# Summing kv in fewer runs, a second place for the last projections, and a new instruction order, in a linear-attention + SoLU feed-forward kernel

## The chip, the cores and the metric

The kernel runs on one core of one Trainium2 chip. The metric is device microseconds (us) of one execution; a run before the change took 510.22 us (median of 3 runs, 509.39 to 512.36). TensorE is called PE, VectorE DVE, ScalarE ACT, GpSimd POOL and SyncE SP, as in the profile. All transfers are issued from SP.

## The reference

Two stages, all in float32 at the interface. Batch 8, 8 heads, sequence 576, head size 64; the hidden width is 1024.

```python
def _attn_ref(q, k, v):
    q_s = softmax(q over the head dimension)        # exp(q - max) / (sum + 1e-9)
    k_s = softmax(k over the sequence)              # the same over 576 positions
    kv = np.einsum('bhsd,bhse->bhde', k_s, v)       # 64 x 64 for each head
    return np.einsum('bhsd,bhde->bhse', q_s, kv)

def _moe_ref(x, w_in, w_out, g_ln):                 # x: 4608 rows of 512
    h = x @ w_in                                    # 4608 x 1024
    e = np.exp(h - max(h)); sm = e / (sum(e) + 1e-9)
    solu = h * sm
    ln = (solu - mean) / np.sqrt(var + 1e-6) * g_ln
    return ln @ w_out                               # 4608 x 512
```

## The kernel before, in words

The sequence of each batch is cut into four full tiles of 128 rows (`C = 4`) and a rest of 64 rows; the rests of two neighbouring batches share one row tile, so there are 36 row tiles for 8 batches. The work is a set of Python generators, each of which issues a few instructions and yields:

- `K0` to `K7` (`keys(b)`): column maxima of k, subtraction, exponential, then the sum kv into one PSUM tile. Its matmuls are `km` by `vm` (128 rows contracted, line 375) and, for the 64 rest rows, `kr` by `vr` (line 377). For each of the four pairs of heads the eight full-tile matmuls are followed at once by the two rest matmuls, and then the generator yields. `largest` transposes a maximum (line 154) and two steps write kv into the block-diagonal weights `bd` (lines 395 and 397). These operands have four bytes per element, and the trace records each such matmul twice.
- `V..` loads v and casts it to `vm`; `Q..a`, `Q..b`, `Q..c` and `R..` make the softmax of q (lines 414 to 432) and transpose it by DMA.
- `w..`, `W` and `y..`, `Z` turn the weights, which arrive as 8-byte numbers, into pairs of float16 (lines 238 to 312).
- `x<t>` (`attend`) multiplies q by `bd`; `h<t>` (`hidden`) is the first feed-forward matmul, 24 matmuls of 128x512 into `h`, of which PSUM holds two, and the row-wise work on it: maximum (DVE line 529), exponential (ACT), small scalars `am`, `pi`, `p`, `ph` (mostly POOL, lines 539 to 548), product (DVE line 551), two halves of `u` (ACT line 556, DVE line 558), its transposition by DMA to `uT`, and the sum of squares (ACT line 565), after which `h` is free.
- `o<t>` (`project`) is the second feed-forward matmul, 24 matmuls of 128x512 into `o`; then DVE or ACT scales it into `os` (lines 601 and 603) and SP stores it. The pool tag `o` has one buffer. The tag `att` has three, used by `x`, `kv` and the transposed maxima. The last row tile is projected in two halves of 256 columns.

The string `ORDER` lists the steps one by one: `h3` runs generator `h3` to its next yield, `K0*2` does that twice, and the ending `.v` gives to DVE the operation that is otherwise POOL's or ACT's (`on(...)`). Each engine and SP work through their instructions in the order in which the list issues them, so an instruction that waits holds up all behind it on its engine. `P` is a step of idle matmuls at the start.

Of the kernel before, what the change touches and what calls it, by code (L numbers as in the profile page):

```python
# [8 lines left out]
F32 = mybir.dt.float32  # L9
# [8 lines left out]
P = 128  # L18
# [66 lines left out]
)  # L85


@with_exitstack
def linear_attention_solu_ffn(ctx: ExitStack, tc: tile.TileContext, q, k, v, w_in, w_out, g_ln, out):

# [6 lines left out]
    nc = tc.nc  # L97
    B, H, S, D = q.shape
# [4 lines left out]
    C = 4  # L103
# [10 lines left out]
    ps = ctx.enter_context(tc.tile_pool(name="ps", bufs=1, space=bass.MemoryType.PSUM))  # L114
# [10 lines left out]
    vm = cst.tile([P, H, C, D + 1], F32, name="vm")  # L125
# [210 lines left out]
    def keys(b):  # L336
# [3 lines left out]
        km = raw["km"]  # L340
# [372 lines left out]
```

## Time and profile before

| | |
|---|---|
| runs shown | 510.22 us median, 509.39 to 512.36 |
| profiled execution, its own time | 510.97 us |
| its span, first to last instruction | 509.2 us |
| PE busy | 463.3 us, 91% of the span |
| DVE busy | 374.5 us, 74% |
| ACT, POOL busy | 279.7 us, 197.5 us |
| DMA | 74.98 MB, 147 GB/s over the span |

Busy time says how long an engine was executing, not whether it set the time. A row of the window view gives, for a stretch of the span, the busy microseconds of each engine and the granted TensorE clock; a row of the timeline view gives start, length, engine, line and operation, with the idle time before it and what ended that in square brackets. Consecutive equal instructions are merged (x16), and the lengths of matmuls overlap, so that the pace of PE is read from starts.

### The profile page before, as it was taken

To read this page: it belongs to the slowest core of one execution; us is meant where nothing else is said; L and a number is where in the kernel's file an instruction comes from. 1 tells how busy PE (TensorE), PEld (TensorE's weight loads), DVE (VectorE), ACT (ScalarE), POOL (GpSimd) and SP (SyncE) were. 2 spreads that over 40 slices of the span, in tenths; PEclk is the share of its full clock that TensorE was granted. 3 is DMA by queue.
4 is the path that set the end of the run, shared out by engine and by line. 5 is a ranking of instruction groups with operands and counts; after the bars stand their busy time and mean duration, and the time that the engine had idled before them with its cause. 6 is when DMAs were issued, how large, how long until landed. Compare 5 with 4: busy or idle time off the path is not lost.

```text
span 509.2 us, 7977 instructions
## 1 busy us (share of the span) xinstructions
PE 463.3 (91%) x2990; PEld 235.3 (46%) x2990; DVE 374.5 (74%) x618; ACT 279.7 (55%) x457; POOL 197.5 (39%) x293
## 2 busy tenths in 40 slices
PE   7357875999999999899999999999999999999986
PEld 2223442445555545454455455545554544444434
DVE  3999999999898989778867777788765464342521
ACT  2657387848557476845547557546656444333400
POOL 3312278457353264753164536326415122020110
PEclk9567997999999999999999999999999999999999
DMA  8896777439996949668729757793626333422251
GB/s 271 246 228 219 220 193 185 103 41 211 213 203 175 217 87 219 139 118 229 161 52 222 205 124 167 149 224 84 132 65 131 74 90 59 103 43 62 60 128 41
DMA packets 159239, 74.98 MB, mean 147 GB/s; under 512 B 127840, under 2 KB 152672, under 8 KB 159200
## 3 DMA queue, kind: packets, MB, share of 16 engines
q1 hardware_dynamic: 159200, 74.47, 62.1%
q8 instruction: 23, 0.38, 0.3%
q14 instruction: 16, 0.13, 0.1%
HBM read 36.70 MB, written 9.44 MB: 91 GB/s over the span
## 4 chain that ended last, share of the span: by engine, by line
PE 59%; DVE 25%; issue 6%; ACT 4%; DMA 3%; POOL 1%; SPq 0%; DVEq 0%; POOLq 0%; ACTq 0%
PE o L593 29%; PE h L522 23%; DVE u L558 3%; PE kv L375 2%; DVE bd L397 2%; DMA w_out<-in_moe_w_out_dram 2%; DVE top L529 1%; DVE qsum L421 1%; DVE qnmx L414 1%; ACT u L556 1%; DMA kr<-in_k_dram 1%; DVE khalf L347 1%; DVE wo L312 1%; DVE iw L242 1%; PE kv L377 1%
## 5 line engine op out<-in xcount | busy, mean ns | idle before, releaser
L522 PE MATMUL h<-wi,xT 128*128 128x512 f16 x864 | 204.9, 384 | 9.5 <-ACT e L565 8.5
L593 PE MATMUL o<-wo,uT 128*128 128x512 f16 (+1 forms) x888 | 200.2, 373 | 4.3 <-DVE os L601 4.1
L522 PEld LDWEIGHTS <-xT 128*128 128x128 f16 x864 | 84.1, 99 | 108.3 <-issue 14.9
L593 PEld LDWEIGHTS <-uT 128*128 128x128 f16 x888 | 85.7, 98 | 99.7 <-issue 5.9
L529 DVE TENSOR_REDUCE top<-h 128x1 f32<-128x1024 f32 x36 | 43.8, 1216 | 33.8 <-PE h L522 33.8
L558 DVE SCALAR_TENSOR_TENSOR u<-h,nmu,u 128x1024 f16<-128x1024 f32 x36 | 46.1, 1280 | 18.3 <-ACT u L556 18.2
L551 DVE SCALAR_TENSOR_TENSOR h<-h,ph,e 128x1024 f32<-128x1024 f32 x36 | 46.3, 1287 | 12.8 <-POOL ph L548 10.7
L539 POOL TENSOR_SCALAR am<-nm 128x1 f32<-128x1 f32 x25 | 9.2, 367 | 111.5 <-ACT nm L531 111.4
L565 ACT ACTIVATE e<-h,nmu 128x1024 f32<-128x1024 f32 x36 | 40.0, 1112 | 19.0 <-DVE u L558 18.9
L556 ACT ACTIVATE u<-h,nmu 128x1024 f16<-128x1024 f32 x36 | 40.0, 1111 | 0.9
L531 ACT ACTIVATE nm<-top,hs 128x1 f32<-128x1 f32 x32 | 9.4, 294 | 55.6 <-DVE top L529 55.4
L535 ACT ACTIVATE e<-h,nm,hs 128x1024 f32<-128x1024 f32 x32 | 38.5, 1203 | 0.8
L432 POOL TENSOR_TENSOR qhl<-qm,qhl 128x1024 f16<-128x1024 f32 (+1 forms) x13 | 28.2, 2169 | 22.2 <-ACT qhl L148 19.4
L553 ACT ACTIVATE nmu<-s 128x1 f32<-128x1 f32 x36 | 7.3, 202 | 52.7 <-DVE h L551 52.6
L578 POOL TENSOR_TENSOR r<-var,mhalf 128x1 f32<-128x1 f32 x36 | 23.2, 649 | 27.4 <-DVE var L575 26.6
L545 POOL TENSOR_TENSOR p<-pi,mone 128x1 f32<-128x1 f32 x36 | 21.7, 602 | 26.1 <-DVE pi L542 24.4
L601 DVE TENSOR_SCALAR os<-o,rr 128x512 f32<-128x512 f32 (+1 forms) x16 | 11.4, 715 | 27.1 <-PE o L593 27.1
L427 POOL TENSOR_TENSOR qm<-qm,qrec 128x1024 f32<-128x1024 f32 x11 | 21.7, 1975 | 20.7 <-DVE qrec L425 14.3
L375 PE MATMUL kv<-vm,km 128*64 128x65 f32 x512 | 23.7, 238 | 5.0 <-ACT vm L148 2.6
L473 PE MATMUL x<-qT,bd 128*128 128x128 f16 x128 | 24.1, 225 | 4.2 <-DVE bd L397 4.2
L375 PEld LDWEIGHTS kv<-vm,km 128*64 128x64 f32 x512 | 19.0, 147 | 14.0 <-issue 4.6
L507 DVE SCALAR_TENSOR_TENSOR xT<-x,xT 128x512 f16<-128x512 f32 x36 | 24.6, 682 | 1.2 <-ACT xT L505 1.2
(137 smaller groups left out, 663.4 us busy)
## 6 DMA issues: line engine op xcount, KB each, us to landing
v<-in_v_dram SPq DMA_DIRECT2D x32, 256.0 KB, 3.6
out_dram<-os SPq DMA_DIRECT2D x31, 256.0 KB, 3.2
km<-in_k_dram SPq DMA_DIRECT2D x7, 1024.0 KB, 6.2
qm<-in_q_dram SPq DMA_DIRECT2D x7, 1024.0 KB, 6.3
w_in<-in_moe_w_in_dram SPq DMA_DIRECT2D x8, 512.0 KB, 6.5
w_out<-in_moe_w_out_dram SPq DMA_DIRECT2D x8, 512.0 KB, 5.7
out_dram<-os SPq DMA_DIRECT2D x10, 128.0 KB, 2.4
km<-in_k_dram SPq DMA_DIRECT2D x2, 512.0 KB, 4.4
```

The costliest lines, as they stand in the source:

```text
L375: nc.tensor.matmul(o, km[:, h + i, c], vm[:, h + i, c], start=(c == 0), stop=False)
L432: on(nc.gpsimd).tensor_tensor(lo, x, hi, op=ALU.subtract)
L473: nc.tensor.matmul(acc, al, bh, start=False, stop=True)
L507: nc.vector.scalar_tensor_tensor(xT[:, 1], acc, 1.0 / QS, xT[:, 0], op0=ALU.mult, op1=ALU.subtract)
L522: nc.tensor.matmul(h[:, ns], xT[:, t, kc], wi[:, s, kc, ns], start=(i == 0), stop=(i == len(terms) - 1))
L529: nc.vector.tensor_reduce(top, h, axis=AX.X, op=ALU.max, negate=True)
L535: nc.scalar.activation(e, h, AF.Exp, bias=nm, scale=hs, accum_out=z)
L551: nc.vector.scalar_tensor_tensor(h, h, ph, e, op0=ALU.mult, op1=ALU.mult, accum_out=s1)
L556: nc.scalar.activation(u[:, 0], h, AF.Identity, bias=nmu)
L558: nc.vector.scalar_tensor_tensor(u[:, 1], h, nmu, u[:, 0], op0=ALU.add, op1=ALU.subtract)
L565: nc.scalar.activation(e, h, AF.Square, bias=nmu, accum_out=s2)
L593: nc.tensor.matmul(o, uT[:, j, f], wo[:, s, f, cols], start=(f == 0 and j == 0 and s == 0), stop=(f == NF - 1 and j == 1))
```

## The change

It does three things.

1. `keys`: the full-tile matmuls of four heads are issued together, then those of the other four, then the rest matmuls of all heads: three steps instead of four. The first matmul alone starts the sum.
2. `project`: of the last six row tiles, every other one (and the first half of the very last) takes its `o` from the three `att` buffers instead of the single `o` buffer.
3. `ORDER` is another list: 1721 steps instead of 1728, with 151 endings `.v` instead of 163. Of its table one row of before and one of after stand below. The order in which the weights are loaded, the order of the queries, the interleaving of all steps and the engine of several steps differ.

```diff
 ORDER = (
-    "LK0*3 w3 K0*2 w3 V00 LQ0 K0*3 P*4 K0*3 LQ0 w0*2 K0 w3 V00 K0.v LV0 w3 K0 w3 K0.v w3 K0*2 Q0a Q0b w0 "
...
+    "LK0*3 LQ0 K0*4 LQ0 K0 P*4 K0*2 w3 Q0c w3 K0*4 V00 w3 Q0a Q0a.v V03 V00 K0.v w0*2 Q0a Q0c V01 K0 Q0b "
...
 )
...
-        for h in range(0, H, 2):
-            for c in range(C + 1):
-                for i in range(2):
-                    o = acc[i * D : (i + 1) * D, h // 2]
-                    if c < C:
-                        nc.tensor.matmul(o, km[:, h + i, c], vm[:, h + i, c], start=(c == 0), stop=False)
-                    else:
-                        nc.tensor.matmul(o, kr[rows, h + i], vr[rows, h + i], start=False, stop=True)
-            yield
+        for hs in heads:
+            for h in range(hs.start, hs.stop, 2):
+                for c in range(C):
+                    for i in range(2):
+                        o = acc[i * D : (i + 1) * D, h // 2]
+                        nc.tensor.matmul(o, km[:, h + i, c], vm[:, h + i, c], start=(h == 0 and c == 0), stop=False)
+            yield
+        for h in range(0, H, 2):
+            for i in range(2):
+                o = acc[i * D : (i + 1) * D, h // 2]
+                nc.tensor.matmul(o, kr[rows, h + i], vr[rows, h + i], start=False, stop=(h == H - 2))
+        yield
...
+    LATE = B * S // P - 6
...
-            o = ps.tile([P, w], F32, name=f"o{name}{i}", tag="o", bufs=1)
+            o_tag = "att" if t >= LATE and (t + i) % 2 else "o"
+            o = ps.tile([P, w], F32, name=f"o{name}{i}", tag=o_tag, bufs=3 if o_tag == "att" else 1)
```

First place: PE, the kv sum of batch 1 (tile `kv1`), before. A row `x8` is eight matmuls in a row.

```order
L375 MATMUL kv1_635<-vm_76,km1_299 64x65 x8
L377 MATMUL kv1_635<-vr_77,kr0_100 64x65 x2
L375 MATMUL kv1_635<-vm_76,km1_299 64x65 x8
L377 MATMUL kv1_635<-vr_77,kr0_100 64x65 x2
L375 MATMUL kv1_635<-vm_76,km1_299 64x65 x8
L377 MATMUL kv1_635<-vr_77,kr0_100 64x65 x2
L375 MATMUL kv1_635<-vm_76,km1_299 64x65 x8
L377 MATMUL kv1_635<-vr_77,kr0_100 64x65 x2
```

The same place on PE now, with the row before it and the two behind it.

```order
L526 MATMUL h0_2_571<-wi_67,xT0_2_533 128x512
L376 MATMUL kv1_626<-vm_76,km1_317 64x65 x32
L381 MATMUL kv1_626<-vr_77,kr0_100 64x65 x8
L153 MATMUL kv1_626<-ident_86,mx1_700 128x128
L526 LDWEIGHTS xT0_3_619
```

Eight runs of one kind have become two. In batches 2 to 7 the steps are spread between other matmuls; there the 48 runs have become 15: two runs of full tiles and one of rests in batches 2, 4 and 6, one of each in batches 3, 5 and 7.

Second place: PE where the projection of row tile (7, 0) ends and the next begins, before.

```order
L593 LDWEIGHTS uT7_0_4881
L593 MATMUL o7_00_5155<-wo_68,uT7_0_4881 128x512
L593 LDWEIGHTS uT7_1_4985
L593 MATMUL o7_10_5199<-wo_68,uT7_1_4985 128x512
L593 LDWEIGHTS uT7_1_4985
```

The same engine now, where the projection of row tile (7, 1) in the `o` buffer ends; `o7_20` lies in an `att` buffer and `o7_40` in the `o` buffer.

```order
L600 MATMUL o7_10_5232<-wo_68,uT7_1_4949 128x512
L600 LDWEIGHTS uT7_2_5092
L600 MATMUL o7_20_5214<-wo_68,uT7_2_5092 128x512
L600 LDWEIGHTS uT7_2_5092
L600 MATMUL o7_20_5214<-wo_68,uT7_2_5092 128x512
```

Between two users of the `o` buffer there are now matmuls of a tile in another buffer: six of `o7_20` here, then `o7_40` begins.

Third place: POOL, its first operations on whole tiles, before (`km`: k; `qm`: q; `qhl`: the float16 halves of q).

```order
L358 TENSOR_TENSOR km0_97<-km0_97,kb0_152 128x1024
L416 TENSOR_TENSOR qm0_111<-qm0_111,qnmx0_1_168 128x8x64
L432 TENSOR_TENSOR qhl0_0_229<-qm0_111,qhl0_0_229 128x512
L480 TENSOR_TENSOR hs0_439<-inv_kv0_338,isc_75 128x1
L432 TENSOR_TENSOR qhl0_2_365<-qm0_111,qhl0_2_365 128x8x2x64
L542 TENSOR_SCALAR pi0_0_491<-am0_0_487 128x1
```

And POOL now, from the same start.

```order
L357 TENSOR_TENSOR km0_97<-km0_97,kb0_149 128x1024
L420 TENSOR_TENSOR qm0_102<-qm0_102,qnmx0_2_141 128x8x128
L420 TENSOR_TENSOR qm0_102<-qm0_102,qnmx0_1_172 128x8x64
L431 TENSOR_TENSOR qm0_102<-qm0_102,qrec0_0_184 128x8x64
L431 TENSOR_TENSOR qm0_102<-qm0_102,qrec0_1_240 128x8x64
L436 TENSOR_TENSOR qhl0_0_232<-qm0_102,qhl0_0_232 128x512 x2
L431 TENSOR_TENSOR qm0_102<-qm0_102,qrec0_2_273 128x8x128
L484 TENSOR_TENSOR hs0_421<-inv_kv0_306,isc_75 128x1
L543 TENSOR_SCALAR am0_0_487<-nm0_0_462 128x1
```

Four more operations on whole tiles of the first batch have gone from DVE to POOL; over the program POOL has 62 of them instead of 53.

123 rows, old and new, of the table ORDER are left out of this document.

## Prediction

> **What bounds the kernel now.** I read the page first, then the windows of 20 us, then the waits of PE, then the timeline of PE where the change acts. The windows give, in order, PE, PEld, DVE, ACT and POOL busy, the granted TensorE clock, the DMA share and GB/s.
>
> ```profile
> PE 463.3 (91%) x2990; PEld 235.3 (46%) x2990; DVE 374.5 (74%) x618; ACT 279.7 (55%) x457; POOL 197.5 (39%) x293
> ...
> 20.00:40.00 20.00, 11.91 (x81) 5.95 (x81) 19.48 (x29) 12.11 (x19) 2.91 (x2) 0.62 0.87 240
> 60.00:80.00 20.00, 13.35 (x125) 7.41 (x126) 18.97 (x25) 17.61 (x29) 15.84 (x16) 0.99 0.74 193
> 80.00:100.00 20.00, 16.75 (x83) 7.67 (x83) 19.56 (x35) 15.01 (x28) 12.16 (x14) 0.84 0.69 155
> 140.00:160.00 20.00, 20.00 (x125) 10.66 (x123) 17.92 (x29) 12.10 (x21) 8.34 (x11) 1.00 0.96 222
> 480.00:500.00 20.00, 16.51 (x78) 7.41 (x77) 6.07 (x11) 2.52 (x4) 2.02 (x6) 1.00 0.43 106
> ```
>
> The reader is to see three stages with three limits. Up to some 115 us DVE is busy all the time (19.48, 18.97 and 19.56 of 20) while PE idles a third: DVE sets the pace. From there to 475 us PE is busy 20.00 of 20 at the full clock, apart from single waits: there a microsecond less of matmuls is a microsecond less of time, as long as the others keep up. In the last 30 us PE alone works and still idles 3.5 of 20. The average of 91% tells none of this.
>
> **The kv sums.** The timeline of PE at batch 1, where nothing stands between the runs:
>
> ```profile
> 72.08 0.69 PE L375 MATMUL kv<-vm,km 128*64 128x65 f32 x16
> 72.69 0.33 PE L377 MATMUL kv<-vr,kr 64*64 64x65 f32 x4
> 72.96 0.69 PE L375 MATMUL kv<-vm,km 128*64 128x65 f32 x16
> 73.57 0.33 PE L377 MATMUL kv<-vr,kr 64*64 64x65 f32 x4
> ```
>
> From start to start a run of 8 matmuls (16 records) takes 0.61 us and a run of 2 takes 0.27. Six matmuls more cost 0.34, so one costs 0.057, and each run pays 0.27 - 2 x 0.057 = 0.16 for being a run of its own. The operands switch between 128*64 and 64*64 there, and the price is that of the switch. I take 0.15 us (rounding in the rows allows 0.13 to 0.17).
>
> The 48 runs of batches 2 to 7 become 15 by the order: 33 x 0.15 = 5.0 us off PE. How often kv begins right after other work stays nearly as it was there (15 places before, 14 now), so nothing is added for that. All six batches lie in the stage where PE is full. The 16 runs of batches 0 and 1 become 4, 1.8 us more, but they fall where DVE sets the pace; I count nothing for them, since PE's idle time there covers them. Ends: 4 us if a part turns into waits, 6.5 with the early ones. The sum now completes later relative to its first matmul, and `den` waits for it. Between the end of kv and the transposition of its maximum (line 154) the new order leaves at least 1.8 us of other matmuls in batches 2 to 7, as the old one does at its shortest.
>
> **The last projections.** The waits of PE name the one `o` buffer, and the timeline shows where:
>
> ```profile
> PE h L522 <- ACT e L565: 8.5, 6, 2.6
> PE o L593 <- DVE os L601: 4.1, 5, 0.9
> ...
> 474.71 5.34 PE L593 MATMUL o<-wo,uT 128*128 128x512 f16 x24
> 480.90 5.34 PE L593 MATMUL o<-wo,uT 128*128 128x512 f16 x24 [0.84 <-DVE os L601]
> 487.08 5.34 PE L593 MATMUL o<-wo,uT 128*128 128x512 f16 x24 [0.84 <-DVE os L601]
> 493.32 5.34 PE L593 MATMUL o<-wo,uT 128*128 128x512 f16 x24 [0.90 <-DVE os L601]
> 499.56 2.78 PE L593 MATMUL o<-wo,uT 128*128 128x256 f16 x24 [0.90 <-DVE os L601]
> 502.97 2.78 PE L593 MATMUL o<-wo,uT 128*128 128x256 f16 x24 [0.63 <-DVE os L601]
> ```
>
> Five times the next projection waits until DVE has emptied the buffer. By starts: 474.71 to 502.97 is 28.26 us for four projections and a half. A projection in full flow is 24 x 0.216 = 5.18 (24 matmuls of `h` or `o` that follow each other take that; the 12 from 279.05 in the chain take 2.59), so four and a half are 23.3, and 4.9 are lost. In the new order six matmuls (1.3 us) or more of a tile in another buffer stand between two users of `o`, against the 0.84 to 0.90 of idle time (some 1.0 from start to start). All five waits go: 4.9 us. What is late next is the transposed `uT` of the very last tile:
>
> ```profile
> 279.05 2.59 PE o L593 x12
> ...
> 474.91 1.22 DVE L529 TENSOR_REDUCE top<-h 128x1 f32<-128x1024 f32 x1 [0.75 <-PE h L522]
> 483.52 1.28 DVE L558 SCALAR_TENSOR_TENSOR u<-h,nmu,u 128x1024 f16<-128x1024 f32 x1 [1.10 <-ACT u L556]
> ...
> uT<-u SPq DMA_TRANSPOSE x36, 4.3
> ```
>
> From the maximum of that tile to the end of `u` pass 9.9 us, and 4.3 more until the transposition has landed: 14.2. The new order puts the emptying of `o6_3`, which needs 30 matmuls (6.5 us) first, ahead of `ph` and the product of the last tile on DVE, which I price at 2 us more: about 16.5. Behind the last `h` PE has 90 matmuls, 19.4 us, before it needs that `uT`. It fits by 3 us. Ends: 3 to 4.9 us.
>
> **The start.** By the order, the work that DVE has ahead of the maximum of the sixth row tile (at 115.7 us) shrinks. Its prices:
>
> ```profile
> L427 DVE TENSOR_TENSOR qm<-qm,qrec 128x1024 f32<-128x1024 f32 x4 | 4.9, 1215 | 0.0
> L416 DVE TENSOR_TENSOR qm<-qm,qnmx 128x1024 f32<-128x1024 f32 x6 | 8.7, 1450 | 0.1
> L427 DVE TENSOR_TENSOR qm<-qm,qrec 128x512 f32<-128x512 f32 x2 | 1.3, 687 | 0.0
> L432 DVE TENSOR_TENSOR qhl<-qm,qhl 128x1024 f16<-128x1024 f32 x3 | 3.7, 1223 | 2.9 <-ACT qhl L148 2.9
> L150 DVE COPY vm<-v 128x512 f32<-128x512 f32 x9 | 3.6, 412 | 0.0
> ```
>
> Three of line 427 go (1.2 + 2 x 0.69 = 2.6), one of line 416 (1.2 of its undisturbed length), one half-size of line 432 (0.7, as line 427's), a copy and a cast (0.8); one full-size of line 432 comes (1.2), and small ones give 0.2: 4.3 us less. Most of it goes to POOL, which by then has 20 operations on whole tiles ahead instead of 15. That isn't free, for a DVE instruction beside such a POOL operation is sometimes stretched; POOL's rows stand beside DVE's here, each pair overlapping:
>
> ```profile
> 12.11 3.39 POOL L358 TENSOR_TENSOR km<-km,kb 128x1024 f32<-128x1024 f32 x1 [8.16 <-ACT kb L333]
> 13.21 2.84 DVE L240 TENSOR_SCALAR iw<-iw 128x1024 int32<-128x1024 int32 x1
> 23.13 0.69 DVE L240 TENSOR_SCALAR iw<-iw 128x1024 int32<-128x1024 int32 x1
> ...
> 43.93 0.69 DVE L347 TENSOR_TENSOR khalf<-km 128x512 f32<-128x512 f32 x1
> 45.49 2.77 POOL L432 TENSOR_TENSOR qhl<-qm,qhl 128x1024 f16<-128x1024 f32 x1 [1.87 <-ACT qhl L148]
> 46.80 2.02 DVE L347 TENSOR_TENSOR khalf<-km 128x512 f32<-128x512 f32 x1
> ```
>
> The same instruction takes 0.69 alone and 2.84 or 2.02 beside POOL: 2.2 and 1.3 lost. Up to 115 us I find six such, of which these are the first and the third, some 7 us in all beside 15 operations, 0.5 each. Five more cost 2.5 us; the ends are 0 (none meets) and 11 (all lose the 2.2 of the worst pair). So the start gives 4.3 - 2.5 = 1.8 us, between 4.3 gained and 6.7 lost.
>
> The Trainium skill, "SBUF — State Buffer", section "Who interferes with whom", says that GpSimd and VectorE share one pair of ports, and that whoever issues first holds it and the other blocks fully, for VectorE instructions with two SBUF inputs or in a two-port mode. The pairs above agree, since DVE's long instruction ends when POOL's does; that only some of the 15 cost anything agrees too, by the condition. By the rule alone, with no operation spared, the start would lose and not gain; that is a rival below.
>
> **The sum.** 510.97 (the profiled execution) - 5.0 - 4.9 - 1.8 = 499.3. The median of the runs is 0.75 lower than that execution; I say 499.0, between the two. Waits of PE on `h` (the row of 8.5 above) I leave as they are: from the fourth tile on, the shortest distance between the last matmul of one `h` and the first that takes its buffer again is 9.5 us of matmuls in the new order and 7.8 in the old, and each has four under 11 us.
>
> **The rivals.**
>
> *POOL's gains come back as blocking and late scalars (slower).* POOL carries 62 operations on whole tiles instead of 53. The scalars `am`, `pi`, `p`, `ph` of a tile stand in the same queue, and DVE already waits for them:
>
> ```profile
> L551 DVE SCALAR_TENSOR_TENSOR h<-h,ph,e 128x1024 f32<-128x1024 f32 x36 | 46.3, 1287 | 12.8 <-POOL ph L548 10.7
> L427 POOL TENSOR_TENSOR qm<-qm,qrec 128x1024 f32<-128x1024 f32 x11 | 21.7, 1975 | 20.7 <-DVE qrec L425 14.3
> ```
>
> If each of the 9 more held a tile back by its 1.98 us, `h` would come free later by up to 18 us in all, and PE, whose slack there is small, would wait for it: 499 + 18 = 517. It decides from 12 us of new waits on. Against it: DVE has 12 fewer steps over the program, and POOL is busy 39% only. Chance 0.06.
>
> *The start gains nothing or loses.* If each of the five added operations costs DVE 2.2 us, as the worst pair, the start loses 6.7 where I take 1.8 gained: 499 + 8.5 = 507.5, at the edge of what can be told. For it speaks that the pairs exist at all; against it that 9 of 15 operations cost nothing. Chance 0.10, of which 0.06 are faster. This is the case of the Trainium skill's rule above with no operation spared.
>
> *kv was covered.* Where PE is full, DVE is at 17.92 of 20; if DVE holds PE soon after, the 5.0 vanish into its waits: 504. For it speaks how near the two engines are to each other there. Against it: DVE gets less work there too. Chance 0.12.
>
> *The tail waits for the last `uT`.* If the 16.5 us become 22, PE waits 3 and the tail gives 2: 502. Chance 0.10.
>
> *No visible change*, the list having lost in the middle what kv and the tail win (8 to 12 us of waits): 508 to 512. Chance 0.05.
>
> **How the numbers follow.** My forecast, 499 within 4, has 0.57. With 0.06, 0.12 and 0.10 of the rivals that are still faster it makes 0.85 for faster by over 0.5% (2.6 us, about what a measurement of this kernel can tell from no change). No visible change has 0.04 + 0.05 = 0.09, slower 0.06. The range reaches down to 492 (start at its good end 2.5, early kv 1.5, waits on `h` fewer by 3) and up to 508 (the start at its bad end, 8.5); it leaves out the slower rival and most of no change.
>
> **What would show it.** Lines 376 and 381 in 19 runs of kv in place of 64, each batch 2.6 to 2.9 us of PE instead of 3.5. In the last 30 us no wait of PE on `os`, and four and a half projections in 23.3 us instead of 28.3. The sixth tile's maximum at 112 to 115 us instead of 115.7, with more stretched DVE instructions beside POOL. PE at 20.00 of 20 between 120 and 470. I am wrong if PE's waits on ACT's `e` or DVE's `bd` exceed 20 us together, or if DVE idles at the start for POOL or a load.

## The result, and the profile after

The changed kernel takes 498.01 us (median of 4 runs, 497.43 to 499.19), the kernel before 509.9 beside it (4 runs, 509.39 to 512.36): a ratio of 0.976, with a 95% interval of 0.9724 to 0.9797. It is 12 us faster; forecast were 499.0, between 492 and 508. The profiled execution took 498.03 us, its span 496.2.

The page's busy times and, from the window view of the changed kernel, the stretches that were shown of before, with two more. The columns are PE, PEld, DVE, ACT, POOL, the granted TensorE clock, the DMA share and GB/s.

```profile
PE 456.0 (92%) x2994; PEld 232.4 (47%) x2994; DVE 370.2 (75%) x606; ACT 278.5 (56%) x457; POOL 207.4 (42%) x305
...
20.00:40.00 20.00, 10.35 (x85) 5.64 (x85) 19.27 (x28) 10.46 (x17) 6.93 (x5) 0.73 0.83 218
60.00:80.00 20.00, 11.67 (x113) 6.00 (x112) 18.11 (x25) 16.07 (x26) 16.05 (x18) 0.88 0.79 222
80.00:100.00 20.00, 16.87 (x85) 7.60 (x85) 19.49 (x35) 15.30 (x28) 10.79 (x12) 0.87 0.52 112
140.00:160.00 20.00, 20.00 (x126) 10.62 (x123) 15.99 (x22) 13.18 (x23) 10.28 (x15) 1.00 0.94 187
280.00:300.00 20.00, 18.08 (x112) 9.20 (x110) 19.62 (x30) 8.66 (x14) 11.88 (x23) 1.00 0.69 127
460.00:480.00 20.00, 20.00 (x94) 9.04 (x93) 7.44 (x13) 6.30 (x11) 3.96 (x12) 1.00 0.45 113
```

The reader is to see that the three stages are still there, and that PE's busy time fell by 7.3 us, 463.3 to 456.0, though its matmuls are the same, but for four idle ones more. One row is new in kind: between 280 and 300 us DVE is full (19.62 of 20) and PE, which sets the pace on either side, is not (18.08). In the kernel before, that stretch had PE at 20.00 and DVE at 14.74:

```profile
280.00:300.00 20.00, 20.00 (x114) 10.11 (x113) 14.74 (x21) 11.08 (x20) 10.51 (x19) 1.00 0.69 174
```

The waits of PE in the changed kernel (in total, times, longest):

```profile
PE h L526 <- ACT e L569: 8.7, 4, 5.7
PE kv L153 <- DVE mx L390: 6.9, 2, 5.4
PE kv L376 <- ACT vm L147: 6.6, 2, 3.9
...
PE o L600 <- ACT os L610: 1.4, 1, 1.4
...
PE o L600 <- DVE os L608: 0.6, 2, 0.4
```

The five waits of line 593 on `os` (4.1 us) have gone from the end; of the three that are left on `os` two lie between 284 and 298 us, the third (0.2) at 178. Waits on `bd` are no longer in the list; before, this row stood there:

```profile
PE x L473 <- DVE bd L397: 4.2, 3, 1.6
```

To see where 13 us of span went, I take for each pair of successive PE starts the usual pace of such a matmul as work (0.216 us for 512 columns, 0.108 for 256, kv by its own starts) and the rest as lost:

| us of PE in the profiled execution | before | after | gained |
|---|---|---|---|
| work, all | 436.8 | 429.6 | 7.2 |
| of it kv | 30.2 | 23.1 | 7.1 |
| lost up to 120 us | 56.2 | 56.9 | -0.7 |
| lost, 120 to 300 | 2.5 | 4.2 | -1.7 |
| lost, 300 to 462 | 3.3 | 0.1 | 3.2 |
| lost after 462 | 5.0 | 0.1 | 4.9 |

The gains sum to 12.9, the difference of the spans (509.2 to 496.2). What lies before the first start of PE and after the last, some 5.4 us in both, is not in the table.

**kv.** The timeline of PE at batch 1, the place shown of before:

```profile
70.97 2.09 PE L376 MATMUL kv<-vm,km 128*64 128x65 f32 x64
72.99 0.68 PE L381 MATMUL kv<-vr,kr 64*64 64x65 f32 x16
75.13 0.32 PE L153 MATMUL kv<-ident,mx 128*128 128x128 f32 x1 [1.46 <-DVE mx L390]
```

From 70.97 to the end of the rests at some 73.6 are 2.7 us; before it was 3.5 (72.08 to some 75.7, less a wait of 0.13 within). The 64 records of full tiles (32 matmuls) take 2.02 us from start to start, 0.063 for each matmul, the change to the rests included.

**The end.** The timeline of PE, and of DVE for the last row tile:

```profile
465.35 27.42 PE L600 MATMUL o<-wo,uT 128*128 128x512 f16 x150
```

```profile
465.55 1.22 DVE L533 TENSOR_REDUCE top<-h 128x1 f32<-128x1024 f32 x1 [1.39 <-PE h L526]
...
472.02 0.75 DVE L608 TENSOR_SCALAR os<-o,rr 128x512 f32<-128x512 f32 x1 [3.58 <-PE o L600]
...
475.71 1.28 DVE L562 SCALAR_TENSOR_TENSOR u<-h,nmu,u 128x1024 f16<-128x1024 f32 x1 [1.42 <-ACT u L560]
```

One row of 150 matmuls stands where there were six rows with five gaps. DVE's rows show the price of the order there: the emptying of `o6_3` at 472.02 comes ahead of the product of the last tile, whose `u` is done at 477.0, 11.4 us after its maximum; with 4.3 for the transposition that is 15.7, inside the 19.4 us of matmuls that PE has left.

### The profile page after: what moved, and what is told of

Read it like the earlier page. It is cut to its first block, busy times and chain, and to the rows that moved or that the text cites. A ratio compares the mean times of both kernels' runs of the same rounds, so it can differ in the third digit from the quotient of the medians.

```text
span 496.2 us, 8006 instructions
## 1 busy us (share of the span) xinstructions
PE 456.0 (92%) x2994; PEld 232.4 (47%) x2994; DVE 370.2 (75%) x606; ACT 278.5 (56%) x457; POOL 207.4 (42%) x305
## 4 chain that ended last, share of the span: by engine, by line
PE 73%; DVE 19%; issue 3%; ACT 2%; DMA 1%; POOL 1%; SPq 0%; DVEq 0%; ACTq 0%; POOLq 0%
PE o L600 32%; PE h L526 32%; PE kv L376 3%; DVE u L562 2%; DVE iw L241 1%; DVE qnmx L418 1%; DMA qm<-in_q_dram 1%; PE x L475 1%; PE x L476 1%; PE x L477 1%; DVE h L555 1%; DVE wo L311 1%; DVE top L533 1%; ACT u L560 1%; DVE gw L241 1%
## 5 line engine op out<-in xcount | busy, mean ns | idle before, releaser
L600 PE MATMUL o<-wo,uT 128*128 128x512 f16 (+1 forms) x888 | 197.7, 373 | 2.6 <-ACT os L610 1.4
L533 DVE TENSOR_REDUCE top<-h 128x1 f32<-128x1024 f32 x36 | 43.8, 1217 | 20.9 <-PE h L526 20.5
L549 POOL TENSOR_TENSOR p<-pi,mone 128x1 f32<-128x1 f32 x36 | 23.4, 651 | 55.3 <-DVE pi L546 54.3
L608 DVE TENSOR_SCALAR os<-o,rr 128x512 f32<-128x512 f32 (+1 forms) x17 | 12.2, 717 | 31.9 <-PE o L600 31.9
L431 POOL TENSOR_TENSOR qm<-qm,qrec 128x1024 f32<-128x1024 f32 (+1 forms) x13 | 24.8, 1907 | 14.3 <-DVE qrec L429 11.3
L420 POOL TENSOR_TENSOR qm<-qm,qnmx 128x1024 f32<-128x1024 f32 (+1 forms) x13 | 25.6, 1969 | 8.7 <-DVE qnmx L418 8.5
L436 POOL TENSOR_TENSOR qhl<-qm,qhl 128x1024 f16<-128x1024 f32 (+1 forms) x11 | 21.6, 1963 | 17.7 <-DVE qhl L149 13.0
L610 ACT ACTIVATE os<-o,rr 128x512 f32<-128x512 f32 x20 | 13.7, 685 | 23.1 <-PE o L600 13.7
L582 POOL TENSOR_TENSOR r<-var,mhalf 128x1 f32<-128x1 f32 x36 | 20.1, 562 | 14.0 <-DVE var L579 13.2
```

What stands on the lines that cost most here:

```text
L420: on(nc.gpsimd).tensor_tensor(x, x, wide(nmx), op=ALU.add)
L431: on(nc.gpsimd).tensor_tensor(x, x, wide(rec), op=ALU.mult)
L533: nc.vector.tensor_reduce(top, h, axis=AX.X, op=ALU.max, negate=True)
L600: nc.tensor.matmul(o, uT[:, j, f], wo[:, s, f, cols], start=(f == 0 and j == 0 and s == 0), stop=(f == NF - 1 and j == 1))
```

## The experiments

In e1 to e8 the kernel before ran beside them at 511.31 us, in e9 to e11 at 511.28, in e12 at 511.36. Ratios are to that, with their 95% interval; the changed kernel's are 0.976 (first run) and 0.9757 (e9).

### e1 to e4: what a run of kv costs

All four have the new list and the two places for `o`; two loads of `vr` (batches 0 and 7) are issued a few steps earlier, as the rests need. e1 puts the matmuls of kv in the old order:

```diff
-                for c in range(C):
+                for c in range(C + 1):
...
+                        if c < C:
+                            nc.tensor.matmul(o, km[:, h + i, c], vm[:, h + i, c], ...)
+                        else:
+                            nc.tensor.matmul(o, kr[rows, h + i], vr[rows, h + i], ...)
```

> The changed kernel with the kv matmuls in the old order again: for each pair of heads eight full-tile matmuls and then the two rest matmuls, in two of the three steps; the list of steps is the new one, only the loads of vr of batches 0, 3 and 7 are issued a few steps earlier. Batches 2 to 7 have 48 runs of one kind instead of 15. Theory (each run costs PE 0.15 us where PE is full, the early batches nothing): 498.0 + 5.0 = 503.0. Rival (the kv work was covered by other engines, the gain came from the list): 498 to 499. Rival (the early batches count as well, 1.8 more): 504.8.

Measured: 502.93 us, 0.9846 (0.9827 to 0.9865), span 501.1, kv's PE work 30.4 us. So the order within kv alone, under the new list, is worth 0.0086 to 0.0089 of 511.3 by the ratios, 4.4 to 4.6 us, and 4.9 by the spans; the work differs by 7.3.

e2 keeps the old order but multiplies a full tile once more in place of each rest, so that no operand changes its shape; the sum of the rests is left out of the result:

```diff
-                            nc.tensor.matmul(o, kr[rows, h + i], vr[rows, h + i], ...)
+                            nc.tensor.matmul(o, km[:, h + i, 0], vm[:, h + i, 0], ...)
```

> As the kernel with the old order of the kv matmuls, but each rest matmul is replaced by a repeated full-tile one (the rests are left out of kv and a quarter of the full tiles counted twice), so that the count, the order and the steps stay and the shape never changes inside kv. Theory (the price is that of the switch between 128*64 and 64*64): no runs left, 498.0 or up to 1.5 below. Rival (the price lies in the alternation of tiles, or in waits on vr and kr): 503.

Measured: 495.46 us, 0.9698 (0.9675 to 0.9722), kv's work 22.3 us. Its timeline of PE at batch 1, and e1's:

```profile
69.62 0.64 PE L375 MATMUL kv<-vm,km 128*64 128x65 f32 x16
70.08 0.29 PE L377 MATMUL kv<-vm,km 128*64 128x65 f32 x4
70.20 0.64 PE L375 MATMUL kv<-vm,km 128*64 128x65 f32 x16
```

```profile
70.19 0.69 PE L375 MATMUL kv<-vm,km 128*64 128x65 f32 x16
70.80 0.33 PE L377 MATMUL kv<-vr,kr 64*64 64x65 f32 x4
71.06 0.69 PE L375 MATMUL kv<-vm,km 128*64 128x65 f32 x16
```

The same number of matmuls in the same alternation of lines: 0.58 us from one row of line 375 to the next where the shapes agree, 0.87 where they change twice. A change costs 0.145 us by these rows. The single records show where: at a change the last start of the old kind and the first of the new are 149 ns apart instead of 50, and the next step is 101 instead of 52. In e1 the shape and the tiles change at the same places; e11 parts the two.

e2 also went further than expected: 3.0 to 3.2 us below the changed kernel by the ratios, where up to 1.5 was allowed. kv's work is 0.8 less; the rest is some 3 us less lost time of PE, in the start and between 120 and 300 us above all. Its sixth maximum stands at 113.1 us, within the scatter that the last section tells of; what else lies behind it is not shown.

e3 goes the other way, with 16 runs in a batch (two half runs of four full-tile matmuls and one rest, for each pair of heads):

```diff
+                for j in range(2):
+                    for c in (2 * j, 2 * j + 1):
...
+                    o = acc[j * D : (j + 1) * D, h // 2]
+                    nc.tensor.matmul(o, kr[rows, h + j], vr[rows, h + j], ...)
```

> As the kernel with the old order of the kv matmuls, but cut twice as finely: four full-tile matmuls, one rest, four full-tile, one rest, so 16 runs per batch. The rests are no longer issued in pairs. Theory (0.15 us a run): 48 more runs in batches 2 to 7 are 7.2 us on top of 503.0, so 510.2. Rival (other engines set the pace there): 503 or less.

Measured: 511.82 us, 1.0024 (1.0011 to 1.0038), span 510.3, kv's work 43.8. The 64 more runs added 13.4 us of work and 9 of time: 0.21 us for a run. That is more than the change of shape, since each rest now stands alone, and one rest alone takes as long as two side by side (by single records 0.256 us with its change, a pair 0.263). The direction is the theory's; the size has this second part, which it lacked.

e4 uses the old order in batches 0 and 1 only.

```diff
+        if b < 2:
...
+                    for c in range(C + 1):
...
+        else:
...
+                    for c in range(C):
...
```

> The changed kernel with the old order of the kv matmuls in batches 0 and 1 alone (16 runs instead of 4). Theory (PE's idle time at the start covers it): 498.0, within 0.4. Rival (the runs of the early batches are on the path too): 498.0 + 1.8 = 499.8.

Measured: 499.51 us, 0.979 (0.9766 to 0.9815), the runs from 497.2 to 501.8. The median is near the rival's 499.8, but the scatter doesn't exclude 498.0. The trace points the other way: kv's work is 2.2 us more than in the changed kernel, and the lost time 3.1 less; the span is 495.4. But it is the trace of the fastest of the five runs (497.19). That the early runs fill idle time of PE, as the prediction had it, is better seen in e1: there all runs together, the early ones included, cost 4.4 to 4.9 us and not 6.8. Taken alone, e4 leaves it open.

### e5 to e7: the parts under the old list

e5 is the kernel before with kv grouped, e6 with the two places for `o`, e7 with both. The parts are those of the diff above; in e5 and e7 the rests follow in the step of the last full tiles.

> The kernel before, with its own list of steps, and the kv matmuls grouped: heads 0 to 3 in the second of the four steps, heads 4 to 7 and all rests in the fourth. Batches 2 to 7 have 16 runs instead of 48. Theory (0.15 us a run where PE is full): 509.9 - 4.8 = 505.1. Rival (the grouping alone brings nothing without the new list, since the sums now come later in the list than their steps): 509 to 511.

> The kernel before, with its own list, and two places for o of the last six row tiles. Theory (five waits of the tail go, 4.9 us): 505.0, and no wait of PE on os in the last 30 us. Rival (the wait moves to the last uT or to an att buffer): 507 to 510.

> The kernel before, with its own list, the grouped kv matmuls and the two places for o. Theory (the two parts add, and lie in different stages): 509.9 - 4.8 - 4.9 = 500.2, so that the new list is worth 2.2 us of the 11.9. Rival (the list is most of the change): 504 or more.

Measured: e5 507.81 us, 0.993 (0.9911 to 0.9948); e6 505.51, 0.9896 (0.9878 to 0.9913); e7 501.15, 0.9806 (0.979 to 0.9822). The two places alone give 5.8 us by the medians and 5.5 by the spans (509.2 to 503.7), of which the trace shows 4.9 as the waits at the end. With kv grouped on top 4.4 more come, and the new list on top of both gives the rest, 0.0046 to 0.0049 of 511, some 2.4 us.

e5 falls short: 3.5 where 4.8 was expected, with 6.7 less work (23.5 after 30.2). The waits of PE in e5 (of the rows shown, the first was 8.3 in the kernel before, the second 2.6 with 3.8 more on the load of `vr`, the third 4.2):

```profile
PE kv L154 <- DVE mx L390: 10.6, 3, 6.4
...
PE kv L376 <- ACT vm L148: 6.8, 1, 6.8
PE x L477 <- DVE bd L401: 5.4, 3, 2.7
```

PE loses 72.0 us there, 5.1 more than before: 2.6 between 60 and 120 us, 2.5 between 120 and 300. A part of the grouped kv's gain turned into waits for what follows kv, `mx` and `bd`, and the old list leaves no more work between these and kv than it did. This is the rival "kv was covered", by about a quarter. But it isn't settled for the old list as such: e7 over e6, the same step under the same list, gives 4.4, and e5's profile is of the slowest of its six runs (508.92).

### e8 and e10: the work that went to POOL

Three products of batch 0's queries with their reciprocals (line 431) are DVE's in the kernel before and POOL's in the changed one. e8 gives all three back to DVE, e10 only the two of half size (the first two lines of the diff); the three steps keep their places in the list.

```diff
-    "K0 Q0c Q0b w0 Q0a LV0 Q0a w3 Q0b"
+    "K0 Q0c Q0b w0 Q0a.v LV0 Q0a w3 Q0b"
...
-    "w2 w1 w2*2 Q0b P K0*2 Q0b"
+    "w2 w1 w2*2 Q0b.v P K0*2 Q0b"
...
-    "x0 x1 W K1 Q0c*2 V11 W Q0c.v"
+    "x0 x1 W K1 Q0c.v Q0c V11 W Q0c.v"
```

> The changed kernel with the three products of the queries of batch 0 by their reciprocals on DVE instead of POOL, as the kernel before had them; the list is the same otherwise. Theory (DVE paces the start; each POOL operation taken away saves it 0.5 us of stretching, each product costs it 0.7 or 1.2): the sixth row tile's maximum 2.6 - 1.5 = 1.1 us later, at 116.4 instead of 115.25, and the time 499.1. Rival (POOL's operations cost DVE nothing): 2.6 us later, 500.6. Rival (blocking eats all of it): no change or earlier, 498.0.

Measured: 502.56 us, 0.9839 (0.9815 to 0.9862); the sixth maximum at 119.7 us, 4.5 later than in the changed kernel, the first at 56.7, also 4.5 later. No theory had that. DVE's timeline in e8 tells it:

```profile
45.94 1.22 DVE L429 TENSOR_TENSOR qm<-qm,qrec 128x1024 f32<-128x1024 f32 x1
48.32 1.23 DVE L434 TENSOR_TENSOR qhl<-qm,qhl 128x1024 f16<-128x1024 f32 x1 [1.16 <-ACT qhl L145]
49.46 3.67 DVE L268 SCALAR_TENSOR_TENSOR wi<-iw,s_in,wi 128x1024 f16<-128x1024 f32 x3
```

The whole-tile product waits its turn in DVE's queue until 45.94; POOL, as soon as it was done with the differences before it, had run it at 31.57 in the changed kernel. What needs it is a cast on ACT, which waits for it; the last three `wi` of the first `h` stand behind that cast in ACT's queue, and PE waits 3.40 us for them. The first `h` in the changed kernel and, from its fifth matmul on, in e8:

```profile
45.80 6.38 PE L526 MATMUL h<-wi,xT 128*128 128x512 f16 x24
```

```profile
49.38 7.26 PE L524 MATMUL h<-wi,xT 128*128 128x512 f16 x20 [3.40 <-ACT wi L266]
```

The wait is not all of the 4.5. In e8 the granted clock is 0.50 from 50 to 54 us, in the changed kernel 1.00 from 48 on, so that from start to start 20 matmuls take 7.1 us in e8 and all 24 take 6.5 in the changed kernel. This execution is also the slowest of e8's five (504.61). So the price was not the engine's; it was the place in time, and in this profile in part the clock.

> The changed kernel with only the two half-size products of line 431 for batch 0 (parts a and b of its queries) put on DVE; the third, part c, stays on POOL. Both run at their old place in the list on either engine. If stretching is what they cost DVE from POOL, DVE gets 2 x 0.69 us of own work and loses about 0.7 + 0.7 + 1.6 us of stretching: the sixth maximum comes between 1.6 us earlier and the same, and the time is within 1 us of the run before. If moving work off DVE is what counts, the maximum comes 1.4 us later and the time is 1.4 us more.

Measured: 500.56 us, 0.9787 (0.9762 to 0.9812), the sixth maximum at 115.9: 1.5 us later than in e9 beside it, and the time 1.5 more, at the edge of what the intervals tell. The rival's number, but not for its reason. The stretching that the two products had caused is indeed gone (the instructions beside the first of them, and beside the difference that follows the second, took 1.95 and 1.25 us in e9, 1.23 and 0.68 here, which nearly pays for the 1.38 us of DVE's own work); but the third product, still POOL's, now starts at 36.21 and meets another instruction, which had been undisturbed:

```profile
36.08 0.71 DVE L236 TENSOR_SCALAR iw<-iw 128x1024 int32<-128x1024 int32 x1 [0.95 <-ACT iw L234]
36.83 2.80 DVE L238 SCALAR_TENSOR_TENSOR iw<-w_in,iw 128x1024 int32<-128x1024 int32 x1
...
36.21 2.35 POOL L428 TENSOR_TENSOR qm<-qm,qrec 128x1024 f32<-128x1024 f32 x1
```

A collision of 1.57 us moved and was not saved. At the row of 36.08 DVE, which had been 1.70 us ahead of e9 (the maximum before it stands at 34.28, in e9 at 35.98), also waits 0.95 us for ACT; by the first `h`'s maximum e10 is 0.95 behind (52.98, in e9 52.03).

### e9 and e11: the changed kernel again, and no 64-row matmul in kv

> The changed kernel unchanged, once more, beside the two that follow: 498 on the first chip, 0.976 of the kernel before (0.972 to 0.980). Its sixth maximum stood at 115.25 us; I expect it within 0.7 of that here, which is the scatter against which the next run is read.

Measured: 499.03 us, 0.9757 (0.9732 to 0.9782); the sixth maximum at 114.41, 0.84 earlier than in the first profile, where 0.7 was allowed for scatter.

e11 multiplies the rests over all 128 rows, by a copy of `vr` with zeros in the other batch's half:

```diff
-    vr = cst.tile([P, H, D + 1], F32, name="vr")
+    vrs = [cst.tile([P, H, D + 1], F32, name=f"vr{j}") for j in range(2)]
+    krs = cst.tile([P, H, D], F32, name="krs")
...
-                nc.tensor.matmul(o, kr[rows, h + i], vr[rows, h + i], start=False, stop=(h == H - 2))
+                nc.tensor.matmul(o, kr[:, h + i], vrs[b % 2][:, h + i], start=False, stop=(h == H - 2))
```

> The changed kernel with the rests multiplied over all 128 rows, against a copy of vr that is zero in the other half, so that no 64-row matmul is left in kv; the result is the same. If the price of a run is that of the switch from 128*64 to 64*64 operands, the 8 remaining runs of rests cost 8 x 0.15 us less: kv's PE work goes from 23.05 to 21.7 to 22.3 us, and the time is 0 to 1.4 us less. If what a run costs is the change of tile or of operands' place, kv's work stays at 23.05. A load of the next batch's kr now has to wait for the matmuls of this one's rests, which may add a wait of DVE on kr; its price is open, up to 2 us a pair.

Measured: 500.18 us, 0.9786 (0.9763 to 0.9808), kv's work 23.05: no gain, where up to 1.4 us was expected. The wait on `kr` that was left open is not among DVE's waits. The timeline of PE in e11 at batch 1 and batch 4, and of the changed kernel at batch 4:

```profile
70.39 2.09 PE L382 MATMUL kv<-vm,km 128*64 128x65 f32 x64
72.31 0.64 PE L387 MATMUL kv<-vr,krs 128*64 128x65 f32 x16
...
223.82 0.69 PE L387 MATMUL kv<-vr,krs 128*64 128x65 f32 x16
224.44 0.82 PE L532 MATMUL h<-wi,xT 128*128 128x512 f16 x3
```

```profile
222.80 0.68 PE L381 MATMUL kv<-vr,kr 64*64 64x65 f32 x16
223.41 0.82 PE L526 MATMUL h<-wi,xT 128*128 128x512 f16 x3
```

Where the rests follow the full tiles directly, the change of shape is gone: 1.92 us from start to start instead of 2.02, and by single records 49 ns, then 51, instead of 149 and 101. But in batches 3 to 7 they come behind an `o` or `h` matmul of 128*128, and entering kv from there costs the same with either shape, 0.62 against 0.61 for the row. My 8 x 0.15 counted a saving at every batch; it exists in three, 0.44 us together, and of these two lie where PE has idle time. (kv's sum hides it, since the rests of batches 0 and 3 took 0.27 and 0.38 us longer than in the first profile of the changed kernel; those of batch 3 did so in e9 as well.) So a "run" is any stretch of matmuls of one shape, and a change to the other work between counts too; that work differs in type as well, float16 after float32, and no run parts type and shape. The Trainium skill, "TensorEngine Tiling (Array Packing)", section "Key Properties", says that a change of the tiling mode drains TensorE, and gives no price; e2 and e11 agree, with 0.145 us.

### e12: one emptying earlier

The list's step that empties the `o` buffer of row tile (3, 2), for which PE waits 1.4 us, is moved ahead of two scaled steps of another tile on ACT.

```diff
-    "o15 Q6a Q6c h20*2 h21 h20 Q6a o15 x22"
+    "o15 Q6a Q6c o15 h20*2 h21 h20 Q6a x22"
```

> The changed kernel with one step of the order list moved: the emptying of the o buffer of the tile whose projection ends at 293 us stands on ACT ahead of two scaled steps of another tile (nm and e, lines 535 and 539) and no longer behind them. In the changed kernel PE waited 1.42 us for it (the row ACT os, 296.76 us). If PE sets the pace there, that wait goes and the whole kernel ends 1.4 us earlier: 496.6 beside the changed kernel's 498.0, 0.973 of the kernel before. If DVE sets the pace in that stretch (19.62 of 20 busy), the wait turns up again behind the next thing that DVE owes PE, and the time stays within 0.4 of the changed kernel's.

Measured: 497.65 us, 0.9725 (0.9705 to 0.9745). The ratio is near the 0.973 expected with the wait gone, but its interval overlaps the changed kernel's two, so no gain is shown by time; its trace answers for the rival:

```profile
295.85 1.46 PE L600 MATMUL o<-wo,uT 128*128 128x512 f16 x6
298.81 0.63 PE L322 MATMUL turned<-ident,ktop 128*128 128x128 f32 x4 [1.50 <-DVE z L573]
```

The projection no longer waits, and the next transposition waits 1.50 us instead, until DVE has come past `xT` (297.98) to `z`. Lost time is 60.9 us, as in the changed kernel (61.3 by the table). Between 280 and 300 us DVE sets the pace, as its 19.62 of 20 said.

## Why the prediction was right, and where its terms were off

**kv, 5.0 predicted.** Right, and by its own mechanism. The work fell by 7.1 us (5.0 and the early 1.8 made 6.8); e1, with all runs back, costs 4.4 to 4.9 us and not 6.8, which speaks for the early share as covered; e4 alone leaves that open. The price of 0.15 us a run, read from the rows of the profile before, is 0.145 by e1 and e2, and in e11 it is gone where other tiles of the same shape follow: it is the change of shape. Each batch was to take 2.6 to 2.9 us of PE instead of 3.5; by single records batches 1 to 7 take 2.6 to 2.8. Under the old list the same step gives 3.5 (e5) or 4.4 (e7 over e6); e5's waits on `mx` and `bd`, which the prediction hadn't priced, can account for the lower one, but whether they come with the old list or with that execution is not shown.

**The tail, 4.9 predicted.** Right: 4.9 in the trace, 27.4 us for 150 matmuls without a gap, and 5.5 to 5.8 for e6 as a whole. The last `u` was done 11.4 us after the maximum, where 12.2 were allowed (16.5 less 4.3); the rival of the last `uT` did not come.

**The start, 1.8 predicted.** About right in this pair of profiles, but within their scatter, and not by the milestone named. By the table PE is 1.5 us ahead at 120 us: kv's early work is 2.2 less (as much as e4 adds), 0.7 more is lost. The sixth maximum, for which 112 to 115 us was forecast, stands only 0.5 earlier, at 115.25 instead of 115.73; five more matmuls of `o`, 1.1 us, are done by then. DVE's durations up to it fell from 112.7 to 110.9 us, by the 1.8 of the sum; but its records overlap, and the time in which DVE ran at all fell by 1.0 only, while its idle time rose by 0.5. The stretching was nearly as priced: nine instructions and 11.1 us instead of seven and 8.2, 2.9 more where 2.5 was taken. Over the seven profiles that have the new steps there (the changed kernel, e1 to e4, e9, e12) the sixth maximum has a mean of 114.4, from 113.1 to 115.8; over the four with the old list (before, e5 to e7) 115.4, from 114.4 to 116.4. So some 1.0 us is gained there, and a single pair of profiles can't measure it.

The assumption that DVE work saved ahead of a maximum is time saved holds only in part. The first maximum comes 5.3 us earlier (52.21, before 57.55), the third 0.4 (71.80, before 72.19): much was deferred. The changed kernel's first and sixth maximum with the first product, then the same of before:

```profile
52.21 1.22 DVE L533 TENSOR_REDUCE top<-h 128x1 f32<-128x1024 f32 x1
53.35 1.21 DVE L241 SCALAR_TENSOR_TENSOR gw<-w_out,gw 128x1024 int32<-128x1024 int32 x1
...
58.68 1.29 DVE L555 SCALAR_TENSOR_TENSOR h<-h,ph,e 128x1024 f32<-128x1024 f32 x1
...
115.25 1.22 DVE L533 TENSOR_REDUCE top<-h 128x1 f32<-128x1024 f32 x1
```

```profile
57.55 1.22 DVE L529 TENSOR_REDUCE top<-h 128x1 f32<-128x1024 f32 x1
...
61.13 1.28 DVE L551 SCALAR_TENSOR_TENSOR h<-h,ph,e 128x1024 f32<-128x1024 f32 x1
...
115.73 1.23 DVE L529 TENSOR_REDUCE top<-h 128x1 f32<-128x1024 f32 x1 [0.20 <-PE h L522]
```

Between the first maximum and the product of its tile stand 6.5 us of steps that convert `w_out` and others, where before it was 3.6: the list does them later. A later milestone is no better by itself: the seventh maximum stands 4.1 us earlier (127.10, before 131.22), but with 47 records of PE fewer ahead of it.

**What the sum left out.** The list's larger effect is elsewhere: between 300 and 462 us 3.2 us of PE's waits on `bd` and `e` are gone, between 120 and 300 1.7 came in, most of it where DVE is full (280 to 300). I had left these waits as they are. Together they gave 1.5; less the 0.3 that the start fell short, that is the 1.2 by which the profiled execution stands below the sum (498.03, where 499.27 was added up). Nothing in the prediction forecast it. And 1.5 is no more than one profile can move: in e9, the same kernel, PE lost some 1.4 us more between 120 and 300. "PE at 20.00 of 20 between 120 and 470" was clearly wrong in that one stretch (18.08), and by little in three others (19.39, 19.92 and 19.77).

**The slower rival** (POOL's late scalars) did not come: PE's waits on `e` are 8.7 us, as before, with POOL at 42%. The rule that the prediction took from the Trainium skill, "SBUF — State Buffer", section "Who interferes with whom", agrees with e10: the pair's price moved with the start times. The prediction read from its pairs that DVE's long instruction ends when POOL's does; by the rows it ends 0.55 us later (16.05 after 15.50, 48.82 after 48.26), nearly the 0.69 that it takes alone, as if it ran once POOL was done. By that rule alone the start would have lost; it did not, and DVE's work was less there too.

## What to carry to other kernels

Read a price from neighbouring rows in the profile (the same matmuls with a change of shape between them and without) and count the changes, those to unrelated work included; here a few rows gave 5.0 us, and 4.4 to 4.9 were measured. When a list moves work off the engine that sets the pace, compare several milestones, and count what is done ahead of each: an early one that gains 5 us and a late one that gains 1 means that most of the work was deferred, not saved. And before an operation goes to the other engine, ask when it will run there: its place in the new queue can cost more than its length.

## What the runs showed of the hardware

Kernels with the same steps there put the third maximum either at 70.2 to 70.3 us (e2, e3, e4, e12) or at 71.6 to 71.8 (the changed kernel, e1, e9), which I had not expected. It is one pair of instructions. In the changed kernel, DVE and POOL:

```profile
67.88 2.26 DVE L239 TENSOR_SCALAR gw<-gw 128x1024 int32<-128x1024 int32 x1 [0.27 <-ACT gw L237]
...
67.69 1.90 POOL L431 TENSOR_TENSOR qm<-qm,qrec 128x1024 f32<-128x1024 f32 x1
```

And the same two in e12:

```profile
67.76 0.69 DVE L239 TENSOR_SCALAR gw<-gw 128x1024 int32<-128x1024 int32 x1
...
68.61 2.74 POOL L431 TENSOR_TENSOR qm<-qm,qrec 128x1024 f32<-128x1024 f32 x1
```

If POOL's starts first, DVE's takes 2.25 us; if DVE's does, it takes 0.63 to 0.69, and POOL's 2.74 instead of 1.90. Of the nine profiles with this pair, DVE was the late one in four (with e10) and POOL in five (with e11). A start that differs by 0.2 us so decides over 1.6 us on DVE, the engine that sets the pace there, and by the sixth maximum such kernels lie anywhere between 113.1 and 115.8 us. A difference of that size between two profiles is no sign of the edit under test.

The clock moves too: in the first profile of the changed kernel the 24 matmuls of the third `h` took 7.03 us from 64.01 (granted clock 0.50 between 66 and 68 us), in e9 5.34 from 63.83 at the full clock. The third maximum came at 71.80 and 71.61 all the same, since DVE reached it no earlier.
